# Pooled attention and a SiLU MLP in one kernel: keys and values of two batches loaded by rows instead of by slots

## The chip, the cores and the metric

The kernel runs on one core of a Trainium2 chip. The metric is the device time of one execution in microseconds. Before the change it is 287.23 us, the median of three runs (286.76 to 287.54).

The core's engines are named as in the profile: PE is TensorE (matmuls; PEld its weight loads), DVE is VectorE, ACT is ScalarE, POOL is GpSimd and SP is SyncE. Each has its own queue of instructions. Transfers (DMA) are issued from the queues of SP, ACT and POOL. SBUF is the on-chip memory with 128 partitions ("rows" here), PSUM the accumulator of TensorE.

## What is computed

Keys and values (8 batches, 8 heads, 576 positions, 64 wide) are averaged over groups of 8 positions, which leaves 72 rows for each head. Every query attends to these 72 rows. The result, 4608 tokens by 512, goes through a two-layer MLP with SiLU.

```python
k_p = k.reshape(B, H, Sp, pool, D).mean(axis=3)          # Sp = 72, pool = 8
v_p = v.reshape(B, H, Sp, pool, D).mean(axis=3)
scores = scale * np.matmul(q, k_p.transpose(0, 1, 3, 2))
attn = np.exp(scores - np.max(scores, axis=-1, keepdims=True))
attn = attn / (np.sum(attn, axis=-1, keepdims=True) + 1e-09)
attn_out = np.matmul(attn, v_p)
# ...
x = attn_out.transpose(0, 2, 1, 3).reshape(B * S, H * D)   # 4608 x 512
h = x @ w_in                                               # 512 x 2048
out = (h * (1.0 / (1.0 + np.exp(-h)))) @ w_out             # 2048 x 512
```

## The kernel before

The MLP works in nine tiles of 512 tokens (`t` = 0 to 8). Each tile has an up projection (`up`) and a down projection (`down` in tile 0, `down_quarters` after it). While the MLP works on tile t, the attention of batch `a = t + 1` is done in small pieces between its matmuls. These pieces are called fillers: `f_up.append((24, f))` means that f is recorded after step 24 of the up projection. A step is one matmul of 512 columns, or two of 256. The order recorded is the order on each engine's queue.

From tile 1 on, a part of the up projection and all of the down projection use a scheme with 7 products in place of 8 (Strassen's), with sums of the inputs made on VectorE: `x_sum` of tokens, `w_sum` of weights, `h_sum` of hidden values, and `rr_sb`, `t_sb`, `c_sb` to recombine the products.

Keys and values are summed over 8 positions in two ways. **By slots** (batches 0, 1 and 2): the 576 rows (head, group) of 512 numbers are laid over 128 partitions in four full slots and one half slot. VectorE sums each slot, and small matmuls with columns of an identity matrix ("selection") bring the rows of each head to their places.

```python
def slot_sums(name, j, halves=False):
    raw = row_tiles[name][j]
    dst = rows5[name][:, SA:] if j else rows5[name][:, :SA]
    w = RE // 4 if halves else RE // 2
    while w > D:
        nc.vector.tensor_add(out=raw[..., :w], in0=raw[..., :w], in1=raw[..., w : 2 * w])
        w //= 2
    nc.vector.tensor_add(out=dst, in0=raw[..., :D], in1=raw[..., D : 2 * D])

def select_k(b, a):                       # 12 matmuls for a = 0, 12 for a = 1
    # ...
    for c in range(2):
        for s in range(4):
            for i, n, r, sp, m in segments(4 * a + s):
                nc.tensor.matmul(
                    st["kz_ps"][32 * s : 32 * (s + 1), a, c, sp : sp + m],
                    lhsT=k5[:n, i, c * DH : (c + 1) * DH],
                    rhs=ident[:n, r : r + m], start=True, stop=True,
                )

def copy_k(b, a, copy=nc.vector.tensor_copy):
    copy(out=kz[b % 2][:, a], in_=batches[b]["kz_ps"][:, a])

def select_v(b, a, tag="at"):             # 6 matmuls for a = 0, 6 for a = 1
    # ... st["v_ps"][:SP, h, :] from shifts[...] and v5[...]
def copy_v(b, a, copy=nc.vector.tensor_copy):
    # ... vp from v_ps
```

**By rows** (batches 3 to 7): the 72 groups lie on 72 partitions, and each holds all heads. The first four positions of each group come by one load, the last four are added to them by a second load with an accumulating transfer (`load_rest`). VectorE then adds halves, and for the keys TensorE transposes.

```python
def load_one(b, name):
    st = batches.setdefault(b, {})
    raw = raw_tile(f"{name}_raw", H)
    load_rows(nc.sync, raw, source(b, name)[:, :, :PH])
    st[f"{name}_raw"] = raw

def load_rest(b, name):
    nc.gpsimd.dma_start(
        out=batches[b][f"{name}_raw"], in_=source(b, name)[:, :, PH:], accum_op=ALU.add)

def pool_k(b, stage):                     # stage 0: add_halves, 72 x 1024 fp32
    # ...                                 # stage 1: add_rest twice, 72 x 256 each, into kp
def pool_v(b):                            # add_halves, then add_rest 72 x 512, into vp
    # ...
def k_transpose(b, parts=(0, 1)):
    # ...
    for a in parts:
        for c in range(2):
            nc.tensor.transpose(kT_ps[:, a, c, :], st["kp"][:, a, c].rearrange("k s d -> k (s d)"),
                                ident[:SP, :SP])
    nc.scalar.copy(kz[b % 2][:, a0:a1], kT_ps[:, a0:a1])
```

The up projection of tile 1 and its VectorE work: `G(8)` is a plain group of 128 hidden units (four matmuls of 512 columns, then a SiLU on ScalarE), a digit is a product of the seven, and `h` and `s` are SiLUs of the recombined `c_sb`.

```python
items = (
    G(12, 13, 14, 15) + [(0, "251")] + G(8) + [(0, "43")] + G(9)
    + [(0, "7h6")] + G(10) + [(0, "s")] + G(11, 0, 1, 2, 3)
)
for n in U_X:
    f_up.append((0, lambda n=n: unit_x_sum(t, n)))
for n in (2, 5):
    f_up.append((36 if t > 1 else 45, lambda n=n: hidden_sum(n, 4, 8)))
f_up.append((56, lambda: hidden_sum(6, 4, 8)))
for n, k0 in ((2, 0), (5, 0), (1, 4), (1, 0)):
    f_up.append((64, lambda n=n, k0=k0: hidden_sum(n, k0, k0 + 4)))
# ...
# in stage(): "5": rr_sb = Q + r_sb   "1": t_sb = R - rr_sb   "7": c_sb[0] = P + t_sb
#             "6": c_sb[1] = Q + t_sb   (all on VectorE)
```

The plain groups of the up projection take turns in three PSUM banks (`banks = dict(mm=3, at=5)`): a group can begin when the SiLU of the group three before it has read its bank. In `down_quarters`, the product 2 reads `h_sum[2]`: its second half of rows first, then its first half.

Of the kernel before, what the change touches and what calls it, by code (L numbers as in the profile page):

```python
# [36 lines left out]
def kernel(  # L37
# [9 lines left out]
    nc = tc.nc  # L47
# [43 lines left out]
    def ps_tile(shape, dtype, tag, name):  # L91
# [12 lines left out]

    h_sum = {
        n: singles.tile([128, KQ, NQ], BF16, name=f"h_sum{n}") for n in (1, 2, 5, 6, 7)
    }
    o_sb = [singles.tile([128, 2, d_model], FP32, name=f"o_sb{n}") for n in range(2)]
# [58 lines left out]
    def source(b, name):  # L167
        return (k if name == "k" else v)[b].rearrange("h (sp p) d -> sp h (p d)", p=POOL)
# [5 lines left out]

    def load_one(b, name):
        st = batches.setdefault(b, {})
        raw = raw_tile(f"{name}_raw", H)
        load_rows(nc.sync, raw, source(b, name)[:, :, :PH])
        st[f"{name}_raw"] = raw

    def load_rest(b, name):
# [5 lines left out]
    def add_halves(raw):  # L187
        nc.vector.tensor_add(
            out=raw[:, :, : 2 * D], in0=raw[:, :, : 2 * D], in1=raw[:, :, 2 * D :]
        )  # L190
# [59 lines left out]

    def load_slots(eng, b, name, i0, i1, half=None):
        es = slice(0, RE) if half is None else slice(half * RE // 2, (half + 1) * RE // 2)
        src = (k if name == "k" else v)[b].rearrange("h (sp p) d -> (h sp) (p d)", p=POOL)
        src = src[:, es]
        how = dict(accum_op=ALU.add) if half else {}
        tiles = row_tiles[name]
        w = es.stop - es.start
        if i0 == SLOTS:
            eng.dma_start(
                out=tiles[1][:REST, SLOTS - SA, :w], in_=src[128 * SLOTS :], **how  # L260
            )
        else:
            j = i0 // SA
            eng.dma_start(
                out=tiles[j][:, i0 - SA * j : i1 - SA * j, :w],
                in_=src[128 * i0 : 128 * i1].rearrange("(i r) e -> r i e", r=128), **how
            )

    def slot_sums(name, j, halves=False):
        raw = row_tiles[name][j]  # L270
        dst = rows5[name][:, SA:] if j else rows5[name][:, :SA]
        w = RE // 4 if halves else RE // 2
        while w > D:
            nc.vector.tensor_add(  # L274
                out=raw[..., :w], in0=raw[..., :w], in1=raw[..., w : 2 * w]
            )
            w //= 2
        nc.vector.tensor_add(out=dst, in0=raw[..., :D], in1=raw[..., D : 2 * D])
# [492 lines left out]
    warm_up(2)  # L771
    load_slots(nc.gpsimd, 1, "k", 0, 3)
    load_slots(nc.gpsimd, 1, "k", 3, 4)
    load_slots(nc.gpsimd, 1, "k", 4, 5)
    load_q(1)
    load_w_in(1536, d_ff)
    for c in range(3):
        load_w_out(c)
    load_slots(nc.gpsimd, 1, "v", 0, 3)
    load_slots(nc.gpsimd, 1, "v", 3, 4)  # L780
    load_slots(nc.gpsimd, 1, "v", 4, 5)
    load_w_out(3)

    def load_half_2(name, half):
        for i0, i1 in ((0, SA), (SA, SLOTS), (SLOTS, SLOTS + 1)):
            load_slots(nc.gpsimd, 2, name, i0, i1, half)

    visits = [third(n) for n in range(3)]
    for t in range(NT):
# [42 lines left out]
        if a < B:  # L832
            q_at = [15, 16, 17, 8] if t > 1 else [24, 25, 26, 2] if t else [82, 84, 86, 88]
            if t == 0:
                for j in range(2):
                    f_up.append((44 + 8 * j, lambda j=j: slot_sums("k", j)))
                    f_up.append((72 + 8 * j, lambda j=j: select_k(1, j)))
                    f_up.append((72 + 8 * j, lambda j=j: copy_k(1, j)))
                    f_down.append((20 + 10 * j, lambda j=j: slot_sums("v", j)))
                    f_down.append((37 + 3 * j, lambda j=j: select_v(1, j, "at")))  # L840
                    f_down.append((37 + 3 * j, lambda j=j: copy_v(1, j)))
            elif t == 1:
                for j in range(2):
                    f_up.append((0, lambda j=j: slot_sums("k", j, halves=True)))
                    f_up.append((22, lambda j=j: select_k(2, j)))
                    f_up.append((23, lambda j=j: copy_k(2, j)))
                    f_down.append((8, lambda j=j: slot_sums("v", j, halves=True)))
                    f_down.append((40, lambda j=j: select_v(2, j, "at")))
                    f_down.append((41, lambda j=j: copy_v(2, j)))
            else:  # L850
                f_up.append((22, lambda: k_transpose(a)))
                f_down.append((10, lambda: pool_v(a)))
            for n in range(4):
                f_to = f_down if t and n == 3 else f_up
                f_to.append((q_at[n], lambda n=n: q_transpose(a, n % 2, n // 2)))
            if t == 0:
                f_down.append((0, lambda: load_half_2("k", 0)))
                f_down.append((0, lambda: load_q(2)))
                f_down.append((0, lambda: load_half_2("k", 1)))
                for half in range(2):  # L860
                    f_down.append((31, lambda half=half: load_half_2("v", half)))
                for y in range(2):
# [59 lines left out]
```

The softmax here doesn't subtract the row's maximum and nothing guards it: scores larger than these inputs give would overflow.

## Time and profile before

| | before |
|---|---|
| time, median of 3 | 287.23 us |
| span in the profile | 284.8 us |
| TensorE busy | 278.0 us (98%) |
| VectorE busy | 225.1 us (79%) |
| ScalarE busy | 183.8 us (65%) |
| granted TensorE clock | 1.0 throughout |
| GB/s over the span | 162 |

The profile has a page for the whole execution (busy time of the engines; 40 slices of the span; the chain of work that ended last; groups of instructions by line) and views that answer questions: the chain in order of time, the timeline of one engine, the groups kept apart by shape, the transfers. In a line of a group the columns are line, engine, operation, output<-input and shape, count, then busy us and mean ns of one, then the idle time in front of it. In a timeline they are start us, length us, engine, line, operation, output<-input, count, and in brackets the idle time in front of it and what ended it. TensorE's busy time includes the latency of each matmul, so it can read 98% where the array waits between matmuls; the chain tells more of that.

### The profile page before, as it was taken

The numbers are of one execution on the slowest core, as the hardware profiler recorded it, in microseconds if no ns is written. First come the engines' busy times: TensorE is split into PE (matmuls) and PEld (weight loads), VectorE is DVE, ScalarE is ACT, GpSimd is POOL, SyncE is SP. The second block draws the span as 40 slices with busy tenths as digits, with TensorE's granted clock in tenths as the row PEclk, the third lists the DMA queues.
The fourth block names the chain that finished last, engine by engine and source line by source line (L and its number), as shares of the span: only waits on it lengthen the run. The fifth ranks groups of instructions, "written<-read, shape, count | busy, mean of one in ns | idle before, by whom it ended". The sixth has DMA issues, their size and how long they took to land.

```text
span 284.8 us, 6920 instructions
## 1 busy us (share of the span) xinstructions
PE 278.0 (98%) x2773; PEld 196.0 (69%) x2793; DVE 225.1 (79%) x403; ACT 183.8 (65%) x359; POOL 52.2 (18%) x68
## 2 busy tenths in 40 slices
PE   8989999999999999999999999999999999999995
PEld 3348544465777677767888886677677867787684
DVE  4887854979969796979698969986998686836773
ACT  1577676458656886688568857794779558325700
POOL 8664317402030011101200101054100000000000
PEclk9999999999999999999999999999999999999999
DMA  7999999793849565964895396839970032005004
GB/s 211 277 266 227 219 306 183 214 199 70 153 69 210 124 96 95 145 148 126 140 177 156 72 147 113 176 59 170 150 142 0 2 85 65 2 9 139 1 3 147
DMA packets 35296, 37.70 MB, mean 132 GB/s; under 512 B 9952, under 2 KB 27616, under 8 KB 35264
## 3 DMA queue, kind: packets, MB, share of 16 engines
q0 software_dynamic: 21760, 20.86, 43.0%
q1 hardware_dynamic: 12928, 15.48, 22.2%
q10 hardware_dynamic: 576, 0.92, 0.9%
q8 instruction: 22, 0.36, 0.6%
q14 instruction: 10, 0.08, 0.1%
HBM read 36.70 MB, written 9.44 MB: 162 GB/s over the span
## 4 chain that ended last, share of the span: by engine, by line
PE 94%; DVE 3%; ACT 1%; issue 1%; DVEq 0%
PE hp_ps L547 25%; PE o_psP L655 15%; PE o_psQ L655 15%; PE u_psQ L488 7%; PE u_psP L488 7%; PE o_psR L655 5%; PE sc_ps L351 4%; PE warm_ps L704 4%; PE o_ps L582 3%; PE nu_ps L395 3%; PE u_psR L488 2%; PE den_ps L369 2%; DVE w_sum L633 1%; PE kz_ps L296 1%; DVE xT L404 1%
## 5 line engine op out<-in xcount | busy, mean ns | idle before, releaser
L547 PE MATMUL hp_ps<-xT,w_in_sb 128*128 128x512 bf16 (+3 forms) x397 | 80.8, 338 | 1.4 <-ACT h_T L553 0.4
L655 PEld LDWEIGHTS <-h_sum 128*128 128x128 bf16 x640 | 60.6, 98 | 11.9 <-issue 1.3
L553 ACT ACTIVATE h_T<-hp_ps 128x512 bf16<-128x512 f32 (+2 forms) x95 | 51.4, 546 | 26.3 <-PE hp_ps L547 24.9
L547 PEld LDWEIGHTS <-w_in_sb 128*128 128x128 bf16 x412 | 39.3, 98 | 25.0 <-issue 1.4
L615 DVE TENSOR_TENSOR h_sum<-h_T 128x1024 bf16<-128x1024 bf16 (+1 forms) x72 | 50.8, 743 | 7.0 <-ACT h_T L553 7.0
L359 ACT ACTIVATE es<-sc_ps 72x384 bf16<-72x384 f32 (+1 forms) x100 | 39.0, 470 | 10.0 <-PE sc_ps L351 9.9
L488 PEld LDWEIGHTS <-w_sum 128*128 128x128 bf16 x300 | 29.4, 98 | 7.7
L655 PEld LDWEIGHTS <-h_T 128*128 128x128 bf16 x256 | 24.1, 98 | 4.4 <-issue 0.9
L404 DVE TENSOR_TENSOR xT<-nu_ps,rec 128x384 bf16<-128x384 f32 (+1 forms) x50 | 24.0, 532 | 0.3
L378 ACT ACTIVATE lnd<-den_ps 128x384 f32<-128x384 f32 (+1 forms) x23 | 11.1, 484 | 20.2 <-PE den_ps L369 20.2
L153 DVE STREAM_TRANSPOSE qT<-q_bf 128x576 bf16<-128x576 bf16 x32 | 23.0, 753 | 0.0
L182 POOL DMA_DIRECT2D raw<-in_k_dram x5 | 7.0, 1398 | 79.2 <-DVE h_sum L615 28.8
L496 ACT ACTIVATE h_T<-c_sb 128x512 bf16<-128x512 f32 x30 | 18.1, 625 | 5.0 <-DVE c_sb L520 5.0
L274 DVE TENSOR_TENSOR raw<-raw 128x384 f32<-128x384 f32 (+3 forms) x20 | 12.4, 618 | 7.5 <-DMA raw<-in_v_dram 4.3
L655 PE MATMUL o_psP<-w_out_sb,h_sum 128*128 128x256 bf16 x128 | 17.6, 273 | 0.0
L655 PE MATMUL o_psQ<-w_sum,h_sum 128*128 128x256 bf16 x128 | 16.7, 273 | 0.0
L655 PE MATMUL o_psQ<-w_out_sb,h_sum 128*128 128x256 bf16 x128 | 16.6, 273 | 0.0
L655 PE MATMUL o_psQ<-w_sum,h_T 128*128 128x256 bf16 x128 | 16.5, 273 | 0.0
L655 PE MATMUL o_psP<-w_sum,h_T 128*128 128x256 bf16 x128 | 16.5, 273 | 0.0
L520 DVE TENSOR_TENSOR c_sb<-u_psP,t_sb 128x512 f32<-128x512 f32 x15 | 10.2, 678 | 7.1 <-PE u_psP L488 3.6
L655 PE MATMUL o_psR<-w_sum,h_sum 128*128 128x256 bf16 x128 | 15.7, 273 | 0.0
L655 PE MATMUL o_psP<-w_sum,h_sum 128*128 128x256 bf16 x128 | 15.4, 272 | 0.0
(77 smaller groups left out, 417.1 us busy)
## 6 DMA issues: line engine op xcount, KB each, us to landing
out_dram<-o_sb SPq DMA_DIRECT2D x128, 64.0 KB, 3.0
q_bf<-in_q_dram POOLq DMA_DIRECT2D x6, 576.0 KB, 11.1
raw<-in_k_dram SPq DMA_DIRECT2D x6, 512.0 KB, 5.0
raw<-in_k_dram POOLq DMA_DIRECT2D x5, 576.0 KB, 9.1
raw<-in_v_dram POOLq DMA_DIRECT2D x5, 576.0 KB, 8.6
raw<-in_v_dram SPq DMA_DIRECT2D x5, 512.0 KB, 7.6
w_in_sb<-in_moe_w_in_dram POOLq DMA_DIRECT2D x8, 256.0 KB, 8.4
w_out_sb<-in_moe_w_out_dram POOLq DMA_DIRECT2D x4, 512.0 KB, 13.5
```

The costliest lines, as they stand in the source:

```text
L153: nc.vector.transpose(out=st["qT"][:, a, f * QF : (f + 1) * QF].rearrange("r i c p -> r (i c p)"), in_=st["q_bf"][:, a, f * n : (f + 1) * n],)
L274: nc.vector.tensor_add(out=raw[..., :w], in0=raw[..., :w], in1=raw[..., w : 2 * w])
L351: nc.tensor.matmul(sc[s][:, cs], lhsT=kz[b % 2][rows, g, c, :], rhs=st["qT"][rows, g, i0:i1, c, :], start=(c == 0), stop=(c == 1),)
L359: nc.scalar.activation(es[:, s, :], sc[s], func=AF.Exp, scale=score_scale)
L404: nc.vector.tensor_mul(out=xT[:, 2 * g0 + c : 2 * (g0 + ng - 1) + c + 1 : 2, cols], in0=nu[c][:, :w].rearrange("r (g n) -> r g n", g=ng), ...
L488: nc.tensor.matmul(ps[bank][:, u, :], lhsT=w[:, kk, 128 * u : 128 * (u + 1)], rhs=x[:, kk, :], start=first and u == 0 and kk == 0, stop=kk ...
L496: nc.scalar.activation(h_T[:, g : g + 2, j * NQ : (j + 1) * NQ], src, func=AF.Silu)
L547: nc.tensor.matmul(hp_ps[:, r0:r1], lhsT=w_in_sb[:, kk, g * 128 : (g + 1) * 128], rhs=xT[:, kk, x0 : x0 + r1 - r0], start=(kk == 0), stop= ...
L553: nc.scalar.activation(h_T[:, g, n0 : n0 + n], hp_ps[:, :n], func=AF.Silu)
L615: nc.vector.tensor_tensor(out=h_sum[n][:, ks, :], in0=quarter(*a, ks), in1=quarter(*b, ks), op=op)
L655: nc.tensor.matmul(ps[b][:, c, :], lhsT=left(n, kt, c), rhs=W_OUT[n][:, kt, :], start=b not in begun, stop=kt == k1 - 1, skip_group_check= ...
L704: nc.tensor.matmul(warm_ps, lhsT=warm[:, :128], rhs=warm, start=True, stop=True)
```

## The change

Batches 1 and 2 are now taken by rows, as batches 3 to 7 are. Only batch 0 stays in slots.

For batch 1 the whole rows (512 numbers for each of 8 heads, on 72 partitions) come in one transfer, into memory that is not yet in use: keys into the buffer of the hidden sums, values into that of the weight sums. One more addition on VectorE (`add_early`, 72 x 2048) makes of them what the accumulating load makes of the others. For batch 2 the two loads by halves stay, but on 72 rows. The selection matmuls, the slot sums and the copies from PSUM of both batches go; two additions of pooling, transposes of keys and a copy on ScalarE come in. The purpose is to take the small matmuls off TensorE. The steps of the fillers change too, among them pool_k(2) at step 24 and k_transpose(2) at step 40 of tile 1's up projection, and the transposes of q in tile 1 are recorded one step later.

```diff
-    h_sum = {
-        n: singles.tile([128, KQ, NQ], BF16, name=f"h_sum{n}") for n in (1, 2, 5, 6, 7)
-    }
+    h_sums = singles.tile([128, 5, KQ, NQ], BF16, name="h_sums")
+    h_sum = {n: h_sums[:, i] for i, n in enumerate((1, 2, 5, 6, 7))}
...
+    early_raw = {
+        n: buf.rearrange("p a k c -> p (a k c)").bitcast(FP32)[:SP, : 2 * H * PH]
+        .rearrange("k (h e) -> k h e", h=H) for n, buf in (("k", h_sums), ("v", w_sum))
+    }
+
+    def load_early(b, name):
+        batches.setdefault(b, {})[f"{name}_raw"] = early_raw[name]
+        nc.gpsimd.dma_start(out=early_raw[name], in_=source(b, name))
+
+    def add_early(b, name):
+        raw = early_raw[name]
+        nc.vector.tensor_add(
+            out=raw[:, :, :PH], in0=raw[:, :, :PH], in1=raw[:, :, PH:]
+        )
...
-    load_slots(nc.gpsimd, 1, "k", 0, 3)
-    load_slots(nc.gpsimd, 1, "k", 3, 4)
-    load_slots(nc.gpsimd, 1, "k", 4, 5)
+    load_early(1, "k")
     load_q(1)
     load_w_in(1536, d_ff)
     for c in range(3):
         load_w_out(c)
-    load_slots(nc.gpsimd, 1, "v", 0, 3)
-    load_slots(nc.gpsimd, 1, "v", 3, 4)
-    load_slots(nc.gpsimd, 1, "v", 4, 5)
+    load_early(1, "v")
     load_w_out(3)
...
-            q_at = [15, 16, 17, 8] if t > 1 else [24, 25, 26, 2] if t else [82, 84, 86, 88]
+            q_at = [15, 16, 17, 8] if t > 1 else [25, 26, 27, 2] if t else [82, 84, 86, 88]
             if t == 0:
-                for j in range(2):
-                    f_up.append((44 + 8 * j, lambda j=j: slot_sums("k", j)))
-                    f_up.append((72 + 8 * j, lambda j=j: select_k(1, j)))
-                    f_up.append((72 + 8 * j, lambda j=j: copy_k(1, j)))
-                    f_down.append((20 + 10 * j, lambda j=j: slot_sums("v", j)))
-                    f_down.append((37 + 3 * j, lambda j=j: select_v(1, j, "at")))
-                    f_down.append((37 + 3 * j, lambda j=j: copy_v(1, j)))
-            elif t == 1:
-                for j in range(2):
-                    f_up.append((0, lambda j=j: slot_sums("k", j, halves=True)))
-                    f_up.append((22, lambda j=j: select_k(2, j)))
-                    f_up.append((23, lambda j=j: copy_k(2, j)))
-                    f_down.append((8, lambda j=j: slot_sums("v", j, halves=True)))
-                    f_down.append((40, lambda j=j: select_v(2, j, "at")))
-                    f_down.append((41, lambda j=j: copy_v(2, j)))
+                f_up.append((44, lambda: add_early(1, "k")))
+                for stage in range(2):
+                    f_up.append((52, lambda stage=stage: pool_k(1, stage)))
+                f_up.append((76, lambda: k_transpose(1)))
+                f_down.append((20, lambda: add_early(1, "v")))
+                f_down.append((30, lambda: pool_v(1)))
             else:
-                f_up.append((22, lambda: k_transpose(a)))
-                f_down.append((10, lambda: pool_v(a)))
+                f_up.append((40 if t == 1 else 22, lambda: k_transpose(a)))
+                if t == 1:
+                    for stage in range(2):
+                        f_up.append((24, lambda stage=stage: pool_k(2, stage)))
+                f_down.append((16 if t == 1 else 10, lambda: pool_v(a)))
...
             if t == 0:
-                f_down.append((0, lambda: load_half_2("k", 0)))
+                f_down.append((0, lambda: load_one(2, "k", nc.gpsimd)))
                 f_down.append((0, lambda: load_q(2)))
-                f_down.append((0, lambda: load_half_2("k", 1)))
-                for half in range(2):
-                    f_down.append((31, lambda half=half: load_half_2("v", half)))
+                f_down.append((0, lambda: load_rest(2, "k")))
+                f_down.append((31, lambda: load_one(2, "v", nc.gpsimd)))
+                f_down.append((31, lambda: load_rest(2, "v")))
```

## The prediction

> **What bounds the kernel now.** I read the page first, for the busiest engine, then the chain that ended last, then that chain in order of time around the lines which the change touches, and last the timelines of single engines there. From the page, parts 1, 2 and 4:
>
> ```profile
> PE 278.0 (98%) x2773; PEld 196.0 (69%) x2793; DVE 225.1 (79%) x403; ACT 183.8 (65%) x359; POOL 52.2 (18%) x68
> PEclk9999999999999999999999999999999999999999
> DMA  7999999793849565964895396839970032005004
> PE 94%; DVE 3%; ACT 1%; issue 1%; DVEq 0%
> ```
>
> TensorE holds 94% of the chain at full clock. So microseconds come off only by taking matmuls from TensorE, and any new wait of TensorE is paid in full. The transfers fill the first seven slices (to about 50 us), the stretch in which batches 1 and 2 are loaded. The chain in order of time shows what the selections of batches 1 and 2 cost (columns: start, length, what):
>
> ```profile
> 28.29 0.21 PE kz_ps L296 x8
> 29.37 0.57 PE kz_ps L296 x8
> 45.48 0.20 PE v_ps L314 x6
> 46.33 0.34 PE v_ps L314 x6
> 58.74 0.67 PE kz_ps L296 x16
> 74.15 0.53 PE v_ps L314 x12
> ```
>
> That is 2.52 us. The timeline of the weight loads adds gaps put down to "issue" at the switches: 0.18 us twice near 28 and 29 us, 0.32 us at 58.67 and 0.16 us after it. Together the 72 small matmuls cost 3.3 us. The third thing to see is VectorE in tile 1, from the first recombination to the sums that open the down projection (timeline, VectorE, and one line of the weight loads):
>
> ```profile
> 58.36 0.69 DVE L508 TENSOR_TENSOR rr_sb<-u_psQ,r_sb 128x512 f32<-128x512 f32 x1 [1.27 <-ACT r_sb L505]
> 59.16 0.69 DVE L511 TENSOR_TENSOR t_sb<-u_psR,rr_sb 128x512 f32<-128x512 f32 x1
> 59.76 0.51 DVE L303 CAST kz<-kz_ps 128x144 bf16<-128x144 f32 x2
> 60.19 2.09 DVE L153 STREAM_TRANSPOSE qT<-q_bf 128x576 bf16<-128x576 bf16 x3
> 62.43 0.69 DVE L520 TENSOR_TENSOR c_sb<-u_psP,t_sb 128x512 f32<-128x512 f32 x1
> 63.04 0.68 DVE L523 TENSOR_TENSOR c_sb<-u_psQ,t_sb 128x512 f32<-128x512 f32 x1
> 63.64 2.43 DVE L633 TENSOR_TENSOR w_sum<-w_out_sb 128x512 bf16<-128x512 bf16 x7
> ...
> 69.47 2.49 DVE L615 TENSOR_TENSOR h_sum<-h_T 128x1024 bf16<-128x1024 bf16 x4
> ...
> 70.20 1.64 PEld L655 LDWEIGHTS <-h_sum 128*128 128x128 bf16 x16 [0.22 <-DVE h_sum L615]
> ```
>
> From 58.36 to 71.9 us VectorE has no gap, and TensorE already waits 0.22 us for it at 70.2. In this one stretch VectorE sets the pace. It idles just before (1.27 us).
>
> [...] at 62.43 the operation on c_sb starts only after three transposes which it does not need. [...]
>
> **The change part by part.** The VectorE costs come from the groups kept apart by shape:
>
> ```profile
> L188 DVE TENSOR_TENSOR raw<-raw 72x1024 f32<-72x1024 f32 x10 | 12.0, 1195 | 0.1
> L193 DVE TENSOR_TENSOR kp<-raw 72x256 bf16<-72x256 f32 x10 | 3.8, 418 | 0.2
> L193 DVE TENSOR_TENSOR vp<-raw 72x512 bf16<-72x512 f32 x5 | 3.4, 687 | 0.2
> ```
>
> Keys of batch 1, tile 0. Removed from TensorE: 0.21 + 0.57 + two gaps of 0.18 = 1.1 us. Added: four transposes. Batch 3's four take from 89.35 to 89.48 before the next matmul starts; I take 0.15 us. But they need kp, and kp now comes late. GpSimd's timeline tells when batch 1's keys land, since each issue waits for the transfer eight before it:
>
> ```profile
> 23.53 0.74 POOL L733 DMA_DIRECT2D w_out_sb<-in_moe_w_out_dram  x1 [1.72 <-DMA raw<-in_k_dram]
> 24.49 1.34 POOL L264 DMA_DIRECT2D raw<-in_v_dram  x2 [0.22 <-DMA raw<-in_k_dram]
> ```
>
> The first three slots landed at 23.5, the fourth near 24.4; the fifth, issued at 14.79 with 9.6 us to landing, also near 24.4. Before, VectorE could begin with the first three at 23.56. Now one semaphore covers all 1,152 KB: the start is 24.5 [...] so about 25.0. Then 2.29 + 1.2 + 0.4 + 0.4, less small overlaps, gives kp at 29.2. TensorE reaches step 76 at about 28.4 (step 72 at 28.04[...]). It waits 0.8 us. The copy of kz moves to ScalarE (0.42 us, from the five of L228) among SiLUs that have little room in the 224-column part; part of that hides in the same wait. Sum: -1.1 + 0.15 + 0.8 = -0.15 us.
>
> Values of batch 1, tile 0. Removed: 0.54 us and gaps, 0.7. In their place VectorE does 2.29 + 1.2 + 0.69, which is 0.4 to 0.5 us more than the six sums (3.3) and the two copies (0.84). Landing at about 41 it ends by 45.3, and the numerators that need it come at 47.7. Nothing waits. Sum: -0.7 us.
>
> Keys of batch 2, tile 1. Removed from TensorE: 0.67 + 0.32 = 1.0 us; added 0.15. Removed from VectorE: the slot sums at 55.5 to 57.1, which lie in front of its 1.27 us of idle time and so are worth nothing, and two copies (59.76 to 60.19, 0.43). Added at step 24, just behind t_sb: pooling, 1195 + 2 x 418 less overlap. The same three instructions in tile 2 run from 83.72 until the next begins at 85.64, so 1.92 us. The contiguous run grows by 1.92 - 0.43 = 1.5 us. The c_sb operations slip, ScalarE waits for them ahead of the SiLUs of the following groups, and with three "mm" banks TensorE stalls; and whatever ScalarE does, the sums for the first half of the second product come 1.5 us later, at 71.6 instead of 70.1. So measured from the tile's start TensorE does not gain 0.85 but loses 1.5. Sum: +1.5 us.
>
> Values of batch 2. Removed 0.53 + 0.1 of gaps; VectorE does 1.9 us instead of 1.49 + 0.74. Sum: -0.6 us.
>
> Transfers: the same bytes, twelve fewer issues on GpSimd. Batch 3's keys now wait for pool_k(2), about 4 us later than at 57.24, but they are needed only at 83.72. No term.
>
> Total: -0.15 - 0.7 + 1.5 - 0.6 = +0.05 us. Tiles 2 to 8 keep their instructions. I say 287.2.
>
> **The rivals.** (a) *TensorE's work alone decides*: then 3.3 - 0.3 = 3.0 us go and the time is 284.2. For it: the 94%. Against it: the gapless VectorE. It would need the c_sb operations to keep their place, but in the order of the changed kernel the pooling and the transposes stand ahead of them. (b) *The new loads are slow*: 72 rows use fewer engines in the stretch where the transfers are already full. If 12 engines took 6 rows each, the keys would land about 3 us late and everything behind them would slip too: 289 to 290. Against it: batches 3 to 7 load 72 rows already, and TensorE does not wait for them. (c) *The loads come earlier and that pays*: they need no free buffer and are fewer. For it: GpSimd waited 6.2 us for batch 2's keys. Against it: the engines were full to 50 us, and no wait of TensorE there is put down to a transfer; 286.5 at most.
>
> **Range and chances.** The parts that I hold firm are the removals of v (-1.3) and the gapless run (+1.5 +/- 0.5). The loose one is batch 1's keys, from -1.0 (data in time) to +1.0 (12 engines). Add 0.5 for the spread of runs and for waits further on: 285.4 to 289.0. Two per cent is 5.7 us, beyond every rival: faster 0.02, same 0.95, slower 0.03.
>
> **What would show it.** In the profile after: TensorE 3 us less busy work but the same span; a wait of TensorE for ScalarE or VectorE near the last groups of tile 1's up projection, and for the h_sum of line 626, of 1.5 us or more in all; c_sb at its old time or later although TensorE is 1 us ahead; a TensorE gap of some 0.8 us before the first kT_ps, ended by kp. If tile 1's up stage is no longer than before (about 14.0 us), the step on VectorE is wrong and rival (a) holds. If the first addition on h_sums starts after 26 us, rival (b). If it starts before 24.3, the wait of 0.8 is wrong.

## The result, and the profile after

The changed kernel takes 294.0 us (median of 6 runs, 292.7 to 295.8), against 287.0 us (6 runs, 286.5 to 287.5) for the kernel before on the same chip. The ratio is 1.025, 95% interval 1.021 to 1.030: 7.0 us slower. The prediction was 287.2 us with a range up to 289.0.

From the page of the kernel after, the same four lines as were read before (busy times, granted clock, share of the DMA engines, chain that ended last):

```profile
PE 278.6 (95%) x2709; PEld 194.4 (66%) x2729; DVE 225.3 (77%) x387; ACT 184.6 (63%) x361; POOL 44.6 (15%) x56
PEclk9999799999999999999999999999999999999999
DMA  7999999687686976983959566739981032005004
PE 64%; DMA 20%; DVE 11%; issue 2%; ACT 1%; POOL 1%; SPq 0%; DVEq 0%; POOLq 0%
```

TensorE has 64 matmuls fewer, yet 0.6 us more of busy time; one slice shows a lower clock. Transfers, which had no part in the chain before, now hold 20% of it, and VectorE 11% instead of 3%. Most of the transfers' part lies in one stretch: from 11.5 to 49.8 us the chain has 9.69 us of a load of w_in and 28.34 us of the load of batch 1's values. VectorE's timeline shows where these transfers are waited for (columns: start, length, what, and in brackets the idle time before it and what ended it):

```profile
28.45 2.29 DVE L194 TENSOR_TENSOR h_sums<-h_sums 72x2048 f32<-72x2048 f32 x1 [4.78 <-DMA h_sums<-in_k_dram]
49.85 2.29 DVE L194 TENSOR_TENSOR w_sum<-w_sum 72x2048 f32<-72x2048 f32 x1 [11.07 <-DMA w_sum<-in_v_dram]
```

The first addition on batch 1's keys starts at 28.45, not at 25.0 as predicted; that on its values at 49.85, not at 41. The first line meets the sign that the prediction gave for its rival (b). TensorE's waits in the kernel after (columns: engine and line, whom it waited for, us in all, times, longest):

```profile
PE kT_ps L239 <- DVE kp L210: 3.8, 1, 3.8
PE o_ps L593 <- DMA w_out_sb<-in_moe_w_out_dram: 1.5, 1, 1.5
PE hp_ps L558 <- ACT h_T L564: 1.5, 2, 1.1
...
PE u_psR L499 <- DVE x_sum L466: 0.9, 1, 0.9
PE o_psP L666 <- DVE h_sums L626: 0.4, 1, 0.4
```

The first two belong to tile 0 and to transfers; the waits for h_T and h_sums are batch 2's, which the prediction had named. After the longest wait the clock falls. The answer by stretches (the columns are named in its own second line):

```profile
core 0: us, PE busy (x) PEld busy (x) DVE busy (x) ACT busy (x) POOL busy (x), PEclk, DMA share, GB/s
30.00:33.00 3.00, 0.40 (x5) 0.28 (x6) 2.93 (x5) 0.00 (x0) 1.55 (x2) 1.00 1.24 217
33.00:38.00 5.00, 4.78 (x23) 2.52 (x22) 5.00 (x12) 2.39 (x6) 0.00 (x0) 0.66 1.21 211
38.00:50.00 12.00, 11.79 (x100) 5.31 (x101) 0.93 (x4) 8.73 (x19) 0.00 (x0) 1.00 1.10 196
```

A mean of 0.66 over 5 us is 3.4 us at half speed. By the trace's record of the clock they begin 1.3 us after the end of the 3.8 us in which TensorE waited; that is an estimate of 1.7 us of lost work.

A good mark for the end of tile 0 is VectorE's first x_sum, which opens tile 1 (first before, then after):

```profile
53.80 1.77 DVE L455 TENSOR_TENSOR x_sum<-xT 128x512 bf16<-128x512 bf16 x5
60.23 1.76 DVE L466 TENSOR_TENSOR x_sum<-xT 128x512 bf16<-128x512 bf16 x5
```

It starts 6.4 us late, nearly the whole loss. So the question is why the same bytes came late. The view of the transfers between 12 and 30 us shows the rate in 40 equal slices of 0.45 us; the last line is one load (KB, and us from issue to landing). First the kernel before, then the one after:

```profile
GB/s 218 187 200 209 205 200 209 198 207 212 198 228 200 191 209 228 357 382 428 410 410 437 266 180 241 211 220 210 193 207 204 203 207 203 200 205 207 209 212 200
...
raw<-in_k_dram POOLq DMA_DIRECT2D x1, 768.0 KB, 9.8
```

```profile
GB/s 209 153 205 212 196 212 205 184 209 207 198 239 198 191 203 207 316 302 212 229 197 220 232 209 216 214 196 225 241 198 232 204 208 210 209 211 205 196 204 207
...
h_sums<-in_k_dram POOLq DMA_DIRECT2D x1, 1152.0 KB, 15.8
```

The weights around them move at some 205 GB/s in both. But the keys, in slots over 128 partitions, moved at 357 to 437 GB/s from 19.2 us on; on 72 partitions, after two slices above 300, at some 200 to 240. In the trace's packet records the median packet of 4096 bytes in this stretch takes 159 ns before and 315 ns after, while the weights' packets of 1024 bytes take 98 ns in both. The DMA share is full to about 50 us, so each of the two slow loads pushes back whatever is behind it.

### The profile page after: what moved, and what is told of

Its sections match the earlier page's. It is cut to its first block, busy times and chain, and to the rows that moved or that the text cites. A ratio compares the mean times of both kernels' runs of the same rounds, so it can differ in the third digit from the quotient of the medians.

```text
span 294.0 us, 6752 instructions
## 1 busy us (share of the span) xinstructions
PE 278.6 (95%) x2709; PEld 194.4 (66%) x2729; DVE 225.3 (77%) x387; ACT 184.6 (63%) x361; POOL 44.6 (15%) x56
## 4 chain that ended last, share of the span: by engine, by line
PE 64%; DMA 20%; DVE 11%; issue 2%; ACT 1%; POOL 1%; SPq 0%; DVEq 0%; POOLq 0%
PE hp_ps L558 16%; PE o_psP L666 13%; PE o_psQ L666 12%; DMA w_sum<-in_v_dram 10%; PE u_psQ L499 6%; PE u_psP L499 6%; PE o_psR L666 4%; DMA raw<-in_k_dram 4%; DMA w_in_sb<-in_moe_w_in_dram 3%; DMA raw<-in_v_dram 2%; PE u_psR L499 2%; DVE w_sum L644 2%; PE sc_ps L362 2%; PE nu_ps L406 2%; DVE h_sums L626 1%
## 5 line engine op out<-in xcount | busy, mean ns | idle before, releaser
L558 PE MATMUL hp_ps<-xT,w_in_sb 128*128 128x512 bf16 (+3 forms) x397 | 82.4, 343 | 2.5 <-ACT h_T L564 1.5
L666 PEld LDWEIGHTS <-h_sums 128*128 128x128 bf16 x640 | 60.7, 98 | 12.3 <-issue 1.3
L626 DVE TENSOR_TENSOR h_sums<-h_T 128x1024 bf16<-128x1024 bf16 (+1 forms) x72 | 50.8, 742 | 7.0 <-ACT h_T L564 7.0
L389 ACT ACTIVATE lnd<-den_ps 128x384 f32<-128x384 f32 (+1 forms) x23 | 11.1, 485 | 19.2 <-PE den_ps L380 19.2
L666 PE MATMUL o_psP<-w_out_sb,h_sums 128*128 128x256 bf16 x128 | 17.6, 273 | 0.4 <-DVE h_sums L626 0.4
L666 PE MATMUL o_psQ<-w_sum,h_sums 128*128 128x256 bf16 x128 | 16.7, 273 | 0.0
L666 PE MATMUL o_psQ<-w_out_sb,h_sums 128*128 128x256 bf16 x128 | 16.6, 273 | 0.0
L199 POOL DMA_DIRECT2D raw<-in_v_dram x6 | 8.4, 1393 | 54.2 <-DMA raw<-in_v_dram 21.5
L593 PE MATMUL o_ps<-w_out_sb,h_T 128*128 128x512 bf16 x61 | 14.5, 380 | 1.8 <-DMA w_out_sb<-in_moe_w_out_dram 1.5
L205 DVE TENSOR_TENSOR raw<-raw 72x1024 f32<-72x1024 f32 x12 | 14.4, 1198 | 2.2 <-DMA raw<-in_k_dram 2.2
L666 PE MATMUL o_psR<-w_sum,h_sums 128*128 128x256 bf16 x128 | 15.5, 273 | 0.0
```

What stands on the lines that cost most here:

```text
L199: nc.gpsimd.dma_start(out=batches[b][f"{name}_raw"], in_=source(b, name)[:, :, PH:], accum_op=ALU.add,)
L205: nc.vector.tensor_add(out=raw[:, :, : 2 * D], in0=raw[:, :, : 2 * D], in1=raw[:, :, 2 * D : 4 * D])
L558: nc.tensor.matmul(hp_ps[:, r0:r1], lhsT=w_in_sb[:, kk, g * 128 : (g + 1) * 128], rhs=xT[:, kk, x0 : x0 + r1 - r0], start=(kk == 0), stop= ...
L593: nc.tensor.matmul(ps, lhsT=h_T[:, g, m * 128 : (m + 1) * 128], rhs=w_out_sb[:, g, :], start=(g == 0), stop=(g == KG - 1),)
L626: nc.vector.tensor_tensor(out=h_sum[n][:, ks, :], in0=quarter(*a, ks), in1=quarter(*b, ks), op=op)
L666: nc.tensor.matmul(ps[b][:, c, :], lhsT=left(n, kt, c), rhs=W_OUT[n][:, kt, :], start=b not in begun, stop=kt == k1 - 1, skip_group_check= ...
```

## The experiments

Four theories were held against each other. **A**: 72 rows are shared by 12 of the 16 DMA engines only. **B**, later **P**: the partitions 0 to 71 are slow to write; P says that a transfer is slow when it writes one half of the 128 partitions alone (0 to 63, or 64 to 127). What in the chip would make it so, no run here shows. **C**: the additions on VectorE, in tile 1 above all, cost the time. **D**: the source, read by heads, is slow. All times are medians; "before" is the kernel before on the same chip.

### Do the transfers' shapes decide? Two other splits, and two changes of what waits

e1_split64, batch 1's rows in two transfers of 64 and 8 rows (64 divides evenly by 16):

```
-        nc.gpsimd.dma_start(out=early_raw[name], in_=source(b, name))
+        load_rows(nc.gpsimd, early_raw[name], source(b, name))   # rows 0-63, 64-71
```

> The early loads of batch 1 (keys, values) each in two transfers, 64 rows and 8 rows, as the later batches' loads from SyncE are; nothing else differs from the changed kernel. Theory A (a transfer of 72 rows is spread over only 12 of the 16 DMA engines, 6 rows each, so it lands late): at most 5 rows on an engine, batch 1's keys land near 25.0 instead of 28.4 us and its values near 42 instead of 49.8; TensorE's wait for kp shrinks from 3.8 to under 1 us; time 288 us. Theory B (72 partitions are slow to write, whatever the engines): the keys land at 28 us again and the time stays at 293 to 294. Theory C (the loss is VectorE's pooling in tile 1): no change in tile 0 matters for it; 292 or more.

e2_heads4, in four transfers of all 72 rows and two heads each:

```
+        for h in range(0, H, 2):
+            nc.gpsimd.dma_start(out=early_raw[name][:, h : h + 2],
+                                in_=source(b, name)[:, h : h + 2])
```

> The early loads of batch 1 each in four transfers of 72 rows by two heads. The rows stay 72, but if each transfer takes 12 engines and the next begins where it ended, four transfers give every engine the same 72 KB. Theory A: every engine's share is even, the keys land near 24.5 to 25.5 us, time 288 us. Theory B (72 partitions are slow): the keys land at 28 us, time 293 to 294. If each transfer began at the same engine, the unevenness would be as before: also 293 to 294.

e3_late_kT, the key transposes of batch 1 later, so that TensorE does not wait for them:

```
-                f_up.append((76, lambda: k_transpose(1)))
+                f_up.append((104, lambda: k_transpose(1)))
```

> The changed kernel with batch 1's key transposes at step 104 instead of 76 of tile 0's up projection, so that TensorE has other work until kp is there at 32.7 us. Theory A: the landings stay late (keys 28.4, values near 49.8), but the wait of 3.8 us and the 3.4 us at half clock behind it go: 3 to 5 us less at the end of tile 0's up projection. The values still land at 49 us, so that part of it is lost again in the down projection, where TensorE then waits longer for vp: time 291 to 293. Theory C: no change, 294.

e4_warm, 17 matmuls that nobody reads in the place of that wait, to keep TensorE's clock up:

```
+                f_up.append((76, lambda: warm_more(17)))
```

> The changed kernel with 17 matmuls whose result nobody reads ahead of batch 1's key transposes (about 3.6 us, as long as the wait there). They bring the transposes no earlier. If the half clock of 3.4 us behind the wait costs its time (3.4 x 0.5 = 1.7 us), keeping TensorE busy saves up to 1.7 us: 292.3. If the transfers set the pace of this part anyway, the half clock lies beside them and nothing is saved: 294.

Measured: e1 293.9 us (before 286.6, ratio 1.025, 1.022 to 1.029), e2 293.2 (1.024, 1.021 to 1.027), e3 296.4 (before 286.6, 1.034, 1.029 to 1.038), e4 295.7 (before 287.0, 1.029, 1.025 to 1.032). In the trace a transfer's semaphore takes 16 counts. In the kernel after, 4 counts of the keys' transfer came at 20.0 to 20.6 us and 12 at 26.6 to 28.4, which fits 12 engines with 6 rows each and 4 with none. In e1 no group of engines is ahead (15 counts of the 64 rows come at 24.8 to 25.9 us, one at 27.5), and in e2 the 16 counts of the last transfer come at 26.3 to 27.7. But the last counts are hardly earlier than before: 28.3 and 27.7. VectorE's first addition in e1:

```profile
28.43 2.29 DVE L194 TENSOR_TENSOR h_sums<-h_sums 72x2048 f32<-72x2048 f32 x1 [5.15 <-DMA h_sums<-in_k_dram]
```

So A does not explain the loss. In e3 and e4, which both came out slower than any of their expectations, TensorE does not wait for kp, and waits elsewhere instead (first e3, then e4):

```profile
PE o_ps L593 <- DMA w_out_sb<-in_moe_w_out_dram: 4.1, 1, 4.1
PE hp_ps L558 <- DMA w_in_sb<-in_moe_w_in_dram: 2.2, 2, 1.8
```

```profile
PE o_ps L593 <- DMA w_out_sb<-in_moe_w_out_dram: 3.4, 1, 3.4
```

These weights were loaded behind batch 1's keys and values. TensorE can be given other work, but then it runs into the next late transfer: the transfers set the pace of tile 0. The half clock comes back there too: 0.57 on average over the 8 us from 50 us in e4, which is 6.9 us at half speed. So e4 does not acquit the clock. Other executions do: those of e1 and e2 whose mean clock was 0.998 and 0.999 took 293.6 and 292.9 us, in the midst of the others of these runs (292.1 to 295.0). Why e3 and e4 are 2.4 and 1.7 us slower than the kernel after was not followed.

### The two batches one by one

e5_batch2_only is the kernel before with batch 2 alone by rows, as in the change; e8_batch1_only is the kernel after with batch 2 in slots again. e7_batch2_early is e5 with two steps moved:

```
-                f_up.append((40 if t == 1 else 22, lambda: k_transpose(a)))
+                f_up.append((22, lambda: k_transpose(a)))
-                        f_up.append((24, lambda stage=stage: pool_k(2, stage)))
+                        f_up.append((0, lambda stage=stage: pool_k(2, stage)))
```

> The kernel before with batch 2 alone by rows (loads of 72 rows, pool_k at step 24 of tile 1, transposes at step 40); batch 1 stays in slots. Theory A: batch 2's data are needed late (59 us), so 12 engines delay nothing that TensorE waits for; what is left is the step of the prediction on VectorE, +1.5 in tile 1's up projection and -0.6 in its down projection: 287.9 us. Theory C (tile 1 is where the 7 us come from): 292 or more.

> The changed kernel with batch 2 again in slots, so batch 1 alone by rows: the complement of batch 2 alone, which took 1.0 us more. If the two parts add up, 293 us, with the same wait of 3.5 to 4 us for kp and values that land near 49 us. If the lateness of batch 1 needs batch 2's loads too (which also use 72 rows and stand behind it in the queue), 289 to 291.

> Batch 2 alone by rows, with pool_k(2) at step 0 instead of 24 of tile 1's up projection and its transposes at step 22 instead of 40. VectorE idles 2.8 us there in the run with pooling at step 24 (behind x_sum, ahead of rr_sb) and the pooling takes 1.9, so the run of VectorE behind t_sb shrinks by 1.9 us. Theory (VectorE's order is what cost batch 2 its gain): TensorE's wait for ScalarE (1.5 us) and for h_sum (0.4) goes, and the 1.6 us of selection matmuls come off: 285.2 to 285.8 against 287.6, and under the kernel before (286.6). If batch 2's data land too late for it (they landed at 55.8 in that run, just as x_sum ended), 286.5.

Measured: e5 287.6 us (before 286.6; ratio 1.0038, 1.0017 to 1.0060), e8 293.4 (before 287.0; 1.023, 1.020 to 1.027), e7 286.9 (before 287.0; 1.0001, 0.998 to 1.002). Batch 1 is the cause of 6.5 us, batch 2 of 1.0. So C falls: with batch 2's pooling in tile 1 alone it expected 292 us or more in e5, and in front of the additions of tile 0 VectorE itself waits for the transfers. In e5 the pooling stands between t_sb (59.41) and c_sb, as predicted, and TensorE waits (VectorE's timeline, then TensorE's waits):

```profile
60.01 1.21 DVE L191 TENSOR_TENSOR raw<-raw 72x1024 f32<-72x1024 f32 x1
61.26 0.75 DVE L196 TENSOR_TENSOR kp<-raw 72x256 bf16<-72x256 f32 x2
61.94 2.08 DVE L153 STREAM_TRANSPOSE qT<-q_bf 128x576 bf16<-128x576 bf16 x3
63.95 0.65 DVE L523 TENSOR_TENSOR c_sb<-u_psP,t_sb 128x512 f32<-128x512 f32 x1
```

```profile
PE hp_ps L550 <- ACT h_T L556: 1.5, 2, 1.1
...
PE o_psP L658 <- DVE h_sum L618: 0.4, 1, 0.4
```

c_sb starts at 63.95 instead of 62.43. In e7 it starts at 62.15 and both waits are as before, yet only level time is reached, 1.1 us over the theory's range: tile 1 ends 1.0 us ahead, and then the pooling of batch 3's keys waits 1.14 us for a transfer and TensorE 1.7 us for x_sum behind it.

e11_batch3_later is e7 with that pooling recorded behind the x_sum of tile 2 (`f_up` 1 of tile 2 in place of `f_down` 100 of tile 1).

> The run with batch 2 alone by rows, pooled at step 0, with one thing more: the pooling of batch 3's keys moves from the end of tile 1 behind the five x_sum operations of tile 2. There VectorE waited 1.1 us for batch 3's keys, with TensorE waiting 1.7 us for x_sum behind it, though tile 1 had ended 1.0 us ahead of before. Theory V (VectorE's order gave that microsecond back): TensorE's wait for x_sum falls from 1.7 to under 0.9 us, and the time is 285.7 to 286.3, 0.2 to 0.4% under before. Rival (something later sets the pace again, as batch 3's keys for its own transposes): the wait for x_sum goes but as much comes back at kT_ps or at c_sb in tile 2, and the time stays at 286.6 to 287.2.

Measured: 287.0 us (before 286.8; ratio 1.0007, 0.999 to 1.003). The rival holds: TensorE's wait for x_sum went, 0.6 us of a wait for rr_sb came, and by the end of tile 2 nothing is left (o_sb at 114.69, before 114.74). Where all of the microsecond went was not followed further.

### The loads alone

e9_loads_alone leaves the whole computation out; its output is zeros. Loads of 1 MB (1.125 MB for 72 rows) run one by one into six layouts:

```
nc.gpsimd.dma_start(out=t[:, :4], in_=slots(b)[:512].rearrange("(i r) e -> r i e", r=128))  # slots, 0-127
nc.gpsimd.dma_start(out=t[:64], in_=slots(b)[:512].rearrange("(i r) e -> r i e", r=64))     # slots, 0-63
nc.gpsimd.dma_start(out=t[:72], in_=rows(b))             # rows, 0-71
nc.gpsimd.dma_start(out=t[:64], in_=rows(b)[:64])        # rows, 0-63
nc.gpsimd.dma_start(out=t[32:96], in_=rows(b)[:64])      # rows, 32-95
nc.gpsimd.dma_start(out=t[64:], in_=rows(b)[:64])        # rows, 64-127
```

> Loads alone, one after the other, nothing beside them; the computation is left out and the output is zeros. Six patterns of keys, twice each: slots on partitions 0 to 127 (1 MB, contiguous in HBM), slots on 0 to 63 (1 MB, contiguous in HBM, 64 rows), rows by heads on 0 to 71 (1.125 MB, as the changed kernel), rows by heads on 0 to 63, on 32 to 95, on 64 to 127 (1 MB each). Theory B, sharpened [...]: slots on 0 to 127 and rows on 32 to 95 land in about 3.5 to 5 us from the issue, all others in 6 to 8. Theory D (the strided source by heads is slow in HBM): slots land fast on 128 and on 64 partitions, and all rows slowly, on 32 to 95 too. Theory A (uneven engines): only the 72 rows are slow.

Measured: 110.6 us in all, in one run. Each load was made twice; the second round, shown here, runs after the stores of the zeros. Its issues on GpSimd, in this order (the name is the buffer's, and the line number tells the layout), and the copies on VectorE that read each load's end:

```profile
59.50 0.78 POOL L65 DMA_DIRECT2D slots<-in_k_dram  x1 [7.52 <-DVE slots L57]
65.82 0.70 POOL L69 DMA_DIRECT2D slots<-in_k_dram  x1 [5.54 <-DVE slots L57]
74.23 0.85 POOL L73 DMA_DIRECT2D rows<-in_k_dram  x1 [7.71 <-DVE rows L57]
84.80 0.70 POOL L77 DMA_DIRECT2D rows<-in_k_dram  x1 [9.72 <-DVE rows L57]
93.10 0.69 POOL L81 DMA_DIRECT2D rows<-in_k_dram  x1 [7.60 <-DVE rows L57]
99.88 0.69 POOL L85 DMA_DIRECT2D rows<-in_k_dram  x1 [6.09 <-DVE rows L57]
```

```profile
65.25 0.14 DVE L60 COPY flag<-slots 32x1 f32<-32x1 f32 x1 [6.05 <-DMA slots<-in_k_dram]
...
73.67 0.14 DVE L60 COPY flag<-slots 32x1 f32<-32x1 f32 x1 [8.15 <-DMA slots<-in_k_dram]
...
84.23 0.14 DVE L60 COPY flag<-rows 32x1 f32<-32x1 f32 x1 [10.30 <-DMA rows<-in_k_dram]
...
92.53 0.14 DVE L60 COPY flag<-rows 32x1 f32<-32x1 f32 x1 [8.03 <-DMA rows<-in_k_dram]
...
99.31 0.14 DVE L60 COPY flag<-rows 32x1 f32<-32x1 f32 x1 [6.51 <-DMA rows<-in_k_dram]
...
107.62 0.14 DVE L60 COPY flag<-rows 32x1 f32<-32x1 f32 x1 [8.03 <-DMA rows<-in_k_dram]
```

From issue to copy: 5.75 us over 128 partitions, 7.85 in slots on 0 to 63, 10.0 for rows on 0 to 71, 7.73 for rows on 0 to 63, 6.21 on 32 to 95, 7.74 on 64 to 127. The same source in the same 64 rows is 1.5 us faster on 32 to 95 than on 0 to 63, and slots on 0 to 63 are as slow as rows there. So D falls, and the order is P's. Its sizes were not met: it expected 3.5 to 5 us over both halves and 6 to 8 on one. While data flow, the view of the transfers has up to 452 GB/s over 128 partitions and mostly 145 to 290 for the slots on 0 to 63. 1 MB in 64 rows or slots on one half takes 7.73 to 7.85 us, and the same on 32 to 95, which lie on both sides of 64, takes 6.21, nearly as fast as 128 partitions (5.75). The 72 rows need 10.0 us for an eighth more bytes, 1.3 us above 9/8 of 7.73: of their 16 counts 4 came by 76.7 us and 12 at 83.3 to 84.1, so A fits as well, but is small.

### The two halves in the kernel itself

e10_both_halves puts batch 1's rows on partitions 0 to 31 and 64 to 103, with zeros between:

```
-        nc.gpsimd.dma_start(out=early_raw[name], in_=source(b, name))
+        for p0, r0, r1 in ((0, 0, 32), (64, 32, 64), (96, 64, SP)):
+            nc.gpsimd.dma_start(out=early_raw[name][p0 : p0 + r1 - r0],
+                                in_=source(b, name)[r0:r1])
```

> The kernel after, with batch 1's 72 rows placed on partitions 0 to 31 and 64 to 103 (transfers of 32, 32 and 8 rows), so on both halves of SBUF; rows 32 to 63 between them are zeros, written early. Keys: the transposes take 104 rows, and the copies to kz pick the 72 columns. Values: two matmuls of 512 columns bring the pooled rows together, and VectorE copies them; that adds about 0.5 us to TensorE and 0.7 to VectorE. [...] Theory P [...]: the median packet of batch 1's keys in 12 to 30 us goes from 340 ns back to about 160 to 190; the addition on h_sums starts by 25.5 us instead of 28.4, that on w_sum by 42.5 instead of 49.0; TensorE's wait for kp falls from 4.2 to at most 1.5 us; the time is 287 to 289.5. Theory D (the source by heads, or whole rows under one semaphore, is slow whatever the partitions): landings within 0.7 us of 28.4 and 49.0, time 293.5 to 295.

Measured: 299.5 us (before 286.8; ratio 1.045, 1.042 to 1.048); the packets stay at 329 ns, the additions start at 29.9 and 51.0. That is outside both expectations. Taken at its word the packets speak against P, but the test did not do what it was meant to: the three transfers follow each other in the queues (GpSimd's issues waited for them until 24.14, 28.35 and 30.07 us), so each still writes one half alone, and the zeros on VectorE held TensorE up by 1.5 us at the start. The rest of the 5.5 us over the kernel after was not followed.

e12_middle therefore puts 64 rows of one transfer on both sides of partition 64, and the last 8 behind them; e13_middle_b1 is the same with batch 2 in slots:

```
+        load_rows(nc.gpsimd, early_raw[name][R0:], source(b, name))   # R0 = 32: 32-95, 96-103
...
+    # pooling and transposes on RP = 104 partitions; 0-31 are zeros
+            v_ps[:SP], lhsT=shifts[:RP, SP + R0 : 2 * SP + R0], rhs=vp_rows,
```

> The kernel after, with batch 1's 72 rows on partitions 32 to 103 (transfers of 64 and 8 rows, as in the run with 64 and 8 rows on partitions 0 to 71). Partitions 0 to 31 of both buffers are zeros: ScalarE writes those of the keys while it has nothing to do at the start, VectorE those of the values in its idle time before the values land. The values are brought to partitions 0 to 71 by one matmul of 512 columns and a copy of VectorE (0.7 us); the transposes take 104 rows. The run with rows on 0 to 31 and 64 to 103 did not decide between the theories: its three transfers go through the queues one after the other, so each still used one half alone. Here the 64 rows of one transfer lie half below and half above partition 64, as in the fourth pattern of the loads alone (6.2 us per MB against 7.7). Theory P: median packet of batch 1's keys in 12 to 30 us 160 to 230 ns instead of 340; addition on h_sums by 26.0 instead of 28.4 us, on w_sum by 43.5 instead of 49.0; the time 287.5 to 290. Theory D (whole rows by heads are slow whatever the partitions, or the share of 16 KB per row): packets over 300 ns, landings within 0.7 us of 28.4 and 49.0, time 293.5 to 296.

> The same placement of batch 1 on partitions 32 to 103, with batch 2 in slots as in the kernel before. Batch 2 by rows cost 1.0 us by itself. Theory P: 286.5 to 289, 1.0 us under the run with both batches by rows, and at best level with the kernel before. Theory D: 292.5 to 295.

Measured: e12 291.9 us (before 286.9; ratio 1.017, 1.015 to 1.019), e13 291.0 (1.016, 1.014 to 1.018). The median packet is back at 159 ns, and the additions start at 26.2 and 44.55: P is right in direction, but the time is 1.9 us above its range, and e13 lies between the ranges of both theories. The rate in e12, 12 to 30 us:

```profile
GB/s 175 155 196 209 212 194 214 198 203 212 230 196 198 196 209 221 341 405 398 419 428 385 293 188 100 98 71 87 113 138 187 224 199 207 204 193 219 203 205 239
```

The 64 rows run at 341 to 428 GB/s, and then the rate falls to 71 to 138 for six slices, 2.7 us. Behind the 64 rows come the 8 on adjacent partitions, 128 KB. e1, with its 8 rows on 64 to 71, has such a fall too, to 77 to 128 GB/s for six slices. The next theory, P carried further, was therefore that 8 adjacent partitions are slower to write than 8 that lie apart; up to here no run had shown it.

e14_spread puts these 8 rows on every fourth partition instead; e15_spread_b1 is the same with batch 2 in slots:

```
+        nc.gpsimd.dma_start(out=early_raw[name][R0:], in_=source(b, name)[:64])
+        nc.gpsimd.dma_start(out=early_raw[name][0:R0:4], in_=source(b, name)[64:])
```

> The run with batch 1's rows on partitions 32 to 103, but its last 8 rows on partitions 0, 4, 8 to 28 instead of 96 to 103; 64 rows on 32 to 95 as there. Both buffers' partitions 0 to 31 are zeroed before (keys by ScalarE, values by VectorE, 3.5 us, most of it in its idle time at the start, perhaps 0.3 us on the path). The copies to kz pick the columns; a second small matmul fetches the 8 rows of the values. Theory P carried further [...]: the fall of the rate to about 100 GB/s behind the 64 rows goes (no more than 1 us under 150 GB/s between 22 and 30 us); the addition on h_sums starts by 25.3 instead of 26.2, that on w_sum by 42.3 instead of 44.6; TensorE waits 0.5 to 1.3 us for kp instead of 2.0; the time 288.3 to 290.5 instead of 291.9. Rival (the fall comes from the load of q or of anything else behind it): the fall stays, landings within 0.4 us of 26.2 and 44.6, 291.3 to 292.8.

> The same with batch 2 in slots as in the kernel before. Theory P carried further: 1.0 us under the run just before, 287.3 to 289.5: level with the kernel before to 1% over it, as the pooling in one piece makes TensorE wait for kp, which takes back the 1.9 us of selections saved. Rival: 290.3 to 292.

Measured: e14 288.3 us (before 286.7; ratio 1.0067, 1.004 to 1.009), e15 287.4 (1.0011, 0.9996 to 1.003). The rate in e14 has no fall, and both additions come early, the first without any wait (rate, then VectorE's timeline):

```profile
GB/s 214 196 207 209 194 214 207 196 214 198 205 205 228 196 198 244 398 387 403 428 437 336 300 245 213 219 210 200 214 192 204 203 214 196 205 212 196 228 209 196
```

```profile
24.03 2.29 DVE L197 TENSOR_TENSOR h_sums<-h_sums 96x2048 f32<-96x2048 f32 x1
...
40.78 2.29 DVE L197 TENSOR_TENSOR w_sum<-w_sum 96x2048 f32<-96x2048 f32 x1 [6.43 <-DMA w_sum<-in_v_dram]
```

TensorE no longer waits for kp. The trace's packet records show the 8 rows directly: the last dozen 4096-byte packets of the keys take 760 to 850 ns each in e12, and 164 to 174 in e14. Bytes, source, pooling and the number of transfers are those of e12. Only 8 rows of each load moved (and with them the place of some zeros, a small matmul and a copy), and the time over the kernel before fell from 5.0 to 1.6 us.

### Both causes out

e16_spread_early is e14 with batch 2 pooled early as in e7; e17_keys_spread is e16 with batch 1's values in slots again.

> The run with the last 8 rows spread on every fourth partition, and batch 2's keys pooled at step 0 of tile 1 instead of 24, transposed at 22 instead of 40: into the 2.8 us in which VectorE there waited for r_sb. Batch 2 by rows cost 1.0 us at its late place and nothing at its early one. Theory (the two causes add up): TensorE's waits for h_T fall from 1.5 to 0.4 us and that for h_sums goes; the time is 286.2 to 287.4, level with before to 0.2% under it. Rival (the transfers of tile 1, which begin later than in the kernel before, give it back): waits for x_sum or w_sum in tile 2, 287.6 to 288.4.

> The run just before with the values of batch 1 in slots, with their sums, selections and copies as in the kernel before, and without the zeros for them. Whole rows of the values save 0.7 us of selections, but cost two matmuls of 512 columns and a wait of 0.2 to 0.7 us for vp_rows, and 0.3 us of VectorE's zeros at the start: so level with the run just before to 0.6 us under it, 285.8 to 287.4. Rival (values by rows were worth their 0.7 us): 0.4 us or more above the run just before.

Measured: e16 287.2 us, before 287.2 on its chip (ratio 1.0005, 0.999 to 1.002); e17 289.1 (1.0076, 1.005 to 1.011). With both causes out e16 is level with the kernel before; nothing tried here beats it. By its number e17 meets its rival (0.4 us or more above e16), but not for the rival's reason: it ends tile 0 ahead of all (table), but batch 2's keys land late for their early place: VectorE waits 3.06 us for them, TensorE 1.6 us for its kT_ps, and its mean clock is 0.992. Why these keys come later than in e16 was not followed.

Summed up, with the start of the two additions, the mark at the end of tile 0, and the time over the kernel before on the same chip (us):

| run | partitions of batch 1's rows | keys | values | x_sum | over before |
|---|---|---|---|---|---|
| before | 0-127 (slots) | 23.56 | 39.65 | 53.80 | 0 |
| after | 0-71 | 28.45 | 49.85 | 60.23 | 7.0 |
| e1_split64 | 0-63, 64-71 | 28.43 | 48.99 | 59.38 | 7.3 |
| e12_middle | 32-95, 96-103 | 26.20 | 44.55 | 56.96 | 5.0 |
| e14_spread | 32-95, every fourth of 0-31 | 24.03 | 40.78 | 53.59 | 1.6 |
| e16_spread_early | the same, batch 2 early | 24.23 | 40.77 | 53.58 | 0.0 |
| e17_keys_spread | the same, keys alone | 23.57 | (slots) | 52.79 | 1.9 |

## Why the prediction was wrong

**The step that failed is "Transfers: the same bytes ... No term", and with it the two landings, 25.0 and about 41.** The missing term measured about 5.7 us. The prediction took the old pieces' rate for granted and added 0.5 us to 24.5, which rested on no measurement. Measured were 28.45 and 49.85. It was the destination that mattered: e1 to e14 changes little but the partitions and takes the excess from 7.3 to 1.6 us. The rate was there to be read: the view of the transfers of the kernel before has the keys at some 410 GB/s between weights at 205, so their spread over 128 partitions was worth something that 72 partitions could lose.

**Keys of batch 1, -0.15.** The chain behind the landing was worked out rightly: 4.3 us from the first addition to kp, and TensorE at the transposes at about 28.4 (in the kernel before, 25 matmuls of 224 columns at 259 ns each take 2.56 us, so they start 0.096 us apart). With the true landing that gives a wait of 28.45 + 4.3 - 28.4 = 4.3 us, where 3.8 was measured and 0.8 predicted; the addition of 72x2048 took 2.29 us, the figure that the prediction had put down for it as an estimate (before, one of 72x1024 took 1.195). Half the clock for 3.4 us behind it had no term at all. With the keys in time (e17) tile 0 ends 1.0 us earlier, the "-1.0 (data in time)" of the range.

**Values of batch 1, -0.7, "Nothing waits".** Wrong in the change: VectorE waited 11.1 us, and w_out, loaded behind the values, held TensorE for 1.5 us. In e16 against e17 whole rows of the values end tile 0 0.8 us later, not earlier, but there with two extra matmuls and a copy; the step as put was not measured with data in time. A slip in it had no effect: VectorE's 2.29 + 1.2 + 0.69 us are level with the 3.3 + 0.84 that go, not 0.4 to 0.5 more.

**Keys and values of batch 2, +1.5 - 0.6 = +0.9.** Right: e5 measured +1.0, with the waits for h_T and h_sum where they were expected. The place in VectorE's order was the reason, as e7 shows; so was the thought that TensorE's saved work alone (rival a, 284.2) buys nothing here.

**Rival (b)** had the sign right and the mechanism mostly wrong: 12 engines with 6 rows each fit the counts, but were worth some 1.3 us of a load alone, and "batches 3 to 7 load 72 rows already, and TensorE does not wait for them" was no argument. That its 3 us for the keys come near the 3.9 measured (28.45 against 24.5) is luck, since e1 and e2, without that unevenness, were as late. That TensorE does not wait for a transfer says nothing of its rate; in the first 50 us, where the queues are full, the rate decides. Whether the later loads on 72 rows hold up others was not tried.

The sum: about 5.7 us for the partitions written (e1 to e14; 2.4 for the 64 rows, 3.3 for the 8), 1.6 for batch 2's place (e14 to e16), which is more than the 1.0 of e5 alone. These are differences of whole times, and from e12 on they carry the layout's own extra work. The range, too, was too narrow by its own parts: their upper ends add up to 289.4 us, not 289.0. That the saved 3.3 us of small matmuls end in level time even in e16 is explained only in part: the layout's own matmuls, copy and zeros take some of it, and 0.8 us come back as a wait for x_sum, as in e7.

## What to carry to other kernels

Before a layout is changed, ask which partitions each transfer writes, not only how many bytes and engines: here a load on partitions 0 to 71 ran at about half the rate (some 200 to 240 GB/s against 357 to 437), and 8 adjacent rows behind a load made the rate fall to 71 to 138. In the first 50 us, where the queues were full, the slow loads were paid for by what stood behind them (w_out, loaded behind the values, held TensorE for 1.5 us), and an engine given other work in the meantime only met the next late transfer (4.1 us in e3). Look at the rate of the loads to be replaced in the profile before, and take it as something that can be lost.

## What the runs showed of the hardware that was not expected

- The same 4096-byte packets took 159 ns (median) when a transfer covers both halves of SBUF, and 312 to 364 ns in the six runs with batch 1's rows on partitions 0 to 71. Two transfers to different halves, one behind the other in the same queues, gained nothing (e10: 329 ns).
- 128 KB on 8 adjacent partitions cost about as much as 1 MB on one half: moving the 8 rows brought the addition on the values forward by 3.8 us (e12 to e14), moving the 64 rows by 4.4 (e1 to e12; in both cases keys and values moved).
- 72 rows in one transfer from GpSimd's queue went to 12 of 16 engines, as far as the times of the 16 counts tell.
- TensorE's clock was at half for 3.4 us near waits of 3.8 us (after), 4.1 us (e3) and 1.6 us (e17), and for 6.8 us near one of 3.4 us (e4). Near the waits of 2.0 us in e12 and 2.7 us in e13 the profiles show full clock. So the length of a wait alone did not tell what the clock would do.
